# Strassen's algorithm for the first product of a fused mLSTM and feed-forward kernel, and the second product's sums by pairs of batches

## Chip, cores, metric

One core of one Trainium2 chip. The metric is device time of one execution in microseconds (us). A profile is one execution; its span is some 1.7 us shorter than the time on the clock.

## The reference

An mLSTM recurrence over 768 steps for 4 batches and 8 heads of 40 gives x, 3072 tokens by 320. A feed-forward block follows:

```python
def _moe_ref(x, w_in, w_out):          # x 3072 x 320, w_in 320 x 2048, w_out 2048 x 320
    h = x @ w_in
    g = h * (1.0 / (1.0 + np.exp(-1.702 * h)))
    return (g @ w_out).astype(np.float32)
```

Everything is f32. The kernel works in six chunks (0 to 5) of 128 steps, so 4 x 128 = 512 tokens each.

## The kernel before

For each chunk the **first product** (`up`) makes 16 tiles of 128 hidden values by 512 tokens: 256 rows of w_in are two full products of 128 rows, the other 64 rows go in pairs, two at a time. GELU takes each tile from PSUM. The **second product** (`down_fast`) uses Strassen's algorithm already: seven block products, called blocks here, for a pair of batches, two pairs, so blocks 0 to 13. The attention of the next chunk is recorded between the blocks.

```python
    def up(w, j, n, between=None, states=False):
        ...
        def full(j, first):
            for c in range(2):
                for i in range(2):
                    f = 2 * j + i
                    T.matmul(ph[j][i][:, ts], w_in_sb[:, c, f * 128:(f + 1) * 128], x[:, c, ts],
                             start=(first and c == 0), stop=(not first and c == 1))
        def rest(j, first):
            for i in range(2):
                r = slice(i * 64, i * 64 + 64)
                T.matmul(ph[j][i][:, ts], w_in_x[r, j, :], x[r, 2, ts], start=first, stop=not first)
        ...
    def hidden_sums(w, js, late):                     # both pairs of batches at once, 512 wide
        for j in js:
            ...
            if late:
                V.tensor_tensor(out=a10, in0=a00, in1=a10, op=OP.subtract)
                V.tensor_tensor(out=s4, in0=a01, in1=s2, op=OP.subtract)
            else:
                V.tensor_tensor(out=s1, in0=a10, in1=a11, op=OP.add)
                V.tensor_tensor(out=s2, in0=s1, in1=a00, op=OP.subtract)

    def down_fast(w, c):
        ...
        def product(a, b, *adds):
            po = ps_m.tile([128, DH], FP, tag="m", name="p_out")     # two PSUM banks in turn
            for f in range(NH):
                T.matmul(po, a(f), b[:, f, :], start=(f == 0), stop=(f == NH - 1))
            for dst, x in adds:                                      # VectorE frees the bank
                ...
        return [lambda: product(block(0, 0), w00, (o00, None)),
                lambda: product(total(2), t2, (o01, o00)),
                lambda: product(block(1, 0), w01, (o10, o01)),
                ...
```

The schedule is manual, and the trace shows VectorE running its instructions in the order in which they are recorded: in chunk 2 its add of block 5, whose product was over when block 6 started at 255.76, runs at 257.46, behind the 2.48 us of multiplications recorded ahead of it. `ps_m` has two banks, so block n+2 can start only when the add of block n is done (in chunk 3 the copy of block 0 ends at 319.48, and block 2 starts at 319.53).

## Time and profile before

| | before |
|---|---|
| time, median of 4 runs (lowest to highest) | 508.4 us (507.69 to 509.11) |
| PE / VectorE (DVE) / ScalarE (ACT) busy | 98% / 52% / 33% |
| chunk 3: first product, then second product with attention | 35.87 us, 44.21 us |

The last row is read from the timeline, as in the prediction, which shows the lines; the next chunk's first L432 matmul starts at 358.67. PE (the matrix engine) is busy 98% of the span and hardly waits, so a change helps if it removes matmul passes and makes no new waits.

### The profile page before, as it was taken

Reading aid. Unit: us, or ns where it says so; the run is one execution under the profiler, and the core shown is the slowest. Engines: PE = TensorE matmul, PEld = TensorE weight load, DVE = VectorE, ACT = ScalarE, POOL = GpSimd, SP = SyncE. Lnnn points to the kernel's source line nnn. Section 1 sums busy time; section 2 is a strip of 40 time slices with the busy share of each in tenths; the row PEclk is TensorE's granted clock in tenths of the full one; section 3 lists DMA queues with packets and bytes.
Section 4 is the critical chain, followed back from the end, with each engine's and each line's share of the span. In section 5 each row is a group of like instructions: output and inputs, shape, how many; then the busy total and the mean of one; then the engine's idle time right before and its main releaser. Section 6 shows DMA issues by size and latency. Waiting matters only on the chain.

```text
span 507.4 us, 9501 instructions
## 1 busy us (share of the span) xinstructions
PE 496.5 (98%) x3838; PEld 352.0 (69%) x3838; DVE 265.1 (52%) x579; ACT 167.6 (33%) x373; POOL 68.6 (14%) x109
## 2 busy tenths in 40 slices
PE   8899999999999999999999999999999999999997
PEld 4774357775448998446999445999644899744797
DVE  6879985872856741418554308465135674003511
ACT  5556766301327301224601113901132720131100
POOL 7250001321001402000322000232000120000000
PEclk9999999999999999999999999999999999999999
DMA  9999799404798403685400593500494000000000
GB/s 149 183 285 285 97 260 175 40 27 77 84 267 87 52 28 65 110 176 65 42 27 14 91 248 48 59 27 1 79 234 37 0 3 28 27 0 0 1 26 27
DMA packets 175692, 44.80 MB, mean 88 GB/s; under 512 B 164353, under 2 KB 170529, under 8 KB 175649
## 3 DMA queue, kind: packets, MB, share of 16 engines
q1 hardware_dynamic: 175648, 44.21, 46.4%
q8 instruction: 30, 0.49, 0.4%
q14 instruction: 14, 0.11, 0.1%
HBM read 40.17 MB, written 4.01 MB: 87 GB/s over the span
## 4 chain that ended last, share of the span: by engine, by line
PE 88%; DVE 7%; POOL 1%; ACT 1%; issue 1%; DVEq 0%; POOLq 0%
PE p_h L432 32%; PE p_out L533 27%; PE p_h L438 9%; PE p_out L479 7%; PE p_o L356 5%; PE p_s L345 4%; PE p_i L362 2%; PE p_x L385 1%; PE p_c L405 1%; DVE s L515 1%; DVE g L514 1%; DVE s L517 1%; DVE w_in_sb L230 1%; DVE s L518 1%; ACT g L443 1%
## 5 line engine op out<-in xcount | busy, mean ns | idle before, releaser
L432 PE MATMUL p_h<-xT,w_in_sb 128*128 128x512 f32 (+1 forms) x400 | 170.7, 580 | 2.1 <-ACT xT L386 1.2
L432 PEld LDWEIGHTS p_h<-xT,w_in_sb 128*128 128x128 f32 x400 | 74.2, 190 | 93.1 <-issue 86.5
L443 ACT ACTIVATE g<-p_h 128x512 f32<-128x512 f32 x96 | 53.5, 599 | 149.8 <-PE p_h L438 83.5
L533 PE MATMUL p_out<-w_out_sb,g 128*128 128x160 f32 x480 | 71.3, 302 | 1.5 <-DVE o_sb L536 1.5
L533 PEld LDWEIGHTS p_out<-w_out_sb,g 128*128 128x128 f32 x480 | 66.6, 190 | 5.8 <-DVE o_sb L536 2.7
L538 DVE TENSOR_TENSOR o_sb<-o_sb,p_out 128x160 f32<-128x160 f32 x70 | 21.5, 319 | 67.3 <-PE p_out L533 66.7
L386 ACT COPY xT<-p_x 128x384 f32<-128x384 f32 x24 | 11.0, 480 | 133.8 <-PE p_x L385 133.8
L517 DVE TENSOR_TENSOR s<-g 128x512 f32<-128x512 f32 x20 | 13.6, 682 | 77.4 <-ACT g L443 77.4
L334 POOL TENSOR_SCALAR_AFFINE_SELECT wt<-wt 128x1024 f32<-128x1024 f32 x24 | 26.6, 1109 | 194.8 <-DMA q_bl<-in_q_dram 101.6
L331 ACT ACTIVATE wt<-wt,cols 128x128 f32<-128x128 f32 x160 | 47.9, 392 | 0.0
L533 PE MATMUL p_out<-t,s 128*128 128x160 f32 x320 | 47.4, 301 | 0.0
L438 PE MATMUL p_h<-xT,w_in_x 64*128 64x512 f32 (+1 forms) x200 | 45.3, 588 | 0.2 <-DVE w_in_x L234 0.2
L533 PEld LDWEIGHTS p_out<-t,s 128*128 128x128 f32 x320 | 44.3, 190 | 0.5
L347 DVE TENSOR_TENSOR wt<-p_s,wt 128x512 f32<-128x512 f32 x48 | 30.5, 684 | 12.7 <-POOL wt L334 8.6
L479 PE MATMUL p_out<-w_out_sb,g 128*128 128x320 f32 x128 | 36.2, 437 | 0.0
L438 PEld LDWEIGHTS p_h<-xT,w_in_x 64*128 64x128 f32 x200 | 18.1, 186 | 22.5 <-issue 17.9
L479 PEld LDWEIGHTS p_out<-w_out_sb,g 128*128 128x128 f32 x128 | 23.8, 190 | 10.1 <-issue 0.5
L356 PE MATMUL p_o<-v_st,wt 128*64 128x41 f32 x768 | 26.8, 230 | 1.4 <-DVE wt L347 1.4
L356 PEld LDWEIGHTS p_o<-v_st,wt 128*64 128x64 f32 x768 | 24.5, 138 | 5.0 <-issue 3.2
L345 PE MATMUL p_s<-qT,kT 40*128 40x128 f32 x384 | 25.8, 280 | 0.4 <-DVE wt L347 0.4
L345 PEld LDWEIGHTS p_s<-qT,kT 40*128 40x128 f32 x384 | 22.7, 187 | 3.1 <-issue 1.1
L409 DVE TENSOR_TENSOR state<-p_c,state 40x328 f32<-40x328 f32 x16 | 7.9, 496 | 30.6 <-PE p_c L405 30.5
(117 smaller groups left out, 503.3 us busy)
## 6 DMA issues: line engine op xcount, KB each, us to landing
wt<-m_row SPq DMA_DIRECT2D x20, 512.0 KB, 6.3
bits<-in_moe_w_in_dram SPq DMA_DIRECT2D x8, 512.0 KB, 8.1
out_dram<-o_sb SPq DMA_DIRECT2D x24, 160.0 KB, 1.8
eo<-in_o_gate_dram SPq DMA_DIRECT2D x5, 640.0 KB, 6.0
v_st<-in_v_dram SPq DMA_DIRECT2D x5, 640.0 KB, 5.7
k_st<-in_k_dram SPq DMA_DIRECT2D x5, 640.0 KB, 11.0
bits<-in_moe_w_out_dram SPq DMA_DIRECT2D x8, 320.0 KB, 5.2
k_bl<-in_k_dram SPq DMA_DIRECT2D x40, 64.0 KB, 2.6
```

Source lines behind the costliest of these rows:

```text
L331: A.activation(out=x[:, h, :], in_=x[:, h, :], func=AF.Exp, scale=-1.0, bias=cols[w][:, b * H + h:b * H + h + 1])
L334: G.affine_select(out=x, in_=x, compare_op=OP.is_ge, fill=0.0, base=0, pattern=[[0, H], [1, L]], channel_multiplier=-1)
L345: T.matmul(pw[i][:, p, :], kT[w, b][r, p, :], qT[w, b][r, p, :], start=True, stop=True)
L347: V.tensor_tensor(out=wt[w, b][:, :, i, :], in0=pw[i], in1=wt[w, b][:, :, i, :], op=OP.mult)
L356: T.matmul(po[t, h, :], wt[w, b][:, p, i, t], v_st[:, b * H + h, :], start=True, stop=True)
L432: T.matmul(ph[j][i][:, ts], w_in_sb[:, c, f * 128:(f + 1) * 128], x[:, c, ts], start=(first and c == 0), stop=(not first and c == 1))
L438: T.matmul(ph[j][i][:, ts], w_in_x[r, j, :], x[r, 2, ts], start=first, stop=not first)
L443: A.activation(out=g[:, i, :], in_=ph[j][i], func=AF.Gelu_apprx_sigmoid)
L479: T.matmul(po, gs[w, f // 2][:, f % 2, b * L:(b + 1) * L], w_out_sb[:, f, :], start=(f == 0), stop=(f == NF - 1))
L517: V.tensor_tensor(out=s1, in0=a10, in1=a11, op=OP.add)
L533: T.matmul(po, a(f), b[:, f, :], start=(f == 0), stop=(f == NH - 1))
L538: V.tensor_tensor(out=dst, in0=x, in1=po, op=OP.add)
```

## The change

Intent: from chunk 2 on, the 256 full rows of the first product go by Strassen's algorithm, seven block products of 128 x 256 columns for eight. Its extra sums go to VectorE and ScalarE. The 24 KB that held the second product's sums now hold three sums of w_in as well, so there is room for one pair of batches' sums at a time: those of the first pair stay in the first product's stage, those of the second pair are made while the first pair's blocks run. The blocks get another order.

```diff
+    def up_fast(w, j, between=None):                       # four tiles a call, two calls a chunk
+        ...
+        product(chain, 0, a00, b00, True)
+        take(0, 0)                                         # ScalarE copies PSUM to g
+        product(other, 0, a01, b10, True)
+        product(chain, 0, as2, bt2)
+        take(0, 1)
+        product(other, 1, as4, b11)
+        product(chain, 0, a10, b01)
+        take(1, 1)
+        product(chain, 1, as1, bt1)
+        for k in js:
+            add(k, 0, 1, chain, 1)                         # VectorE adds PSUM to g
+        ...  # 64 rest rows, in pairs
+        for k in js:
+            add(k, 0, 0, other, 0)
+            add(k, 0, 1, other, 1)
+            A.activation(out=g[k][0], in_=g[k][0], func=AF.Gelu_apprx_sigmoid)
+        product(chain, 0, a11, bt4)
+        for k in js:
+            A.activation(out=g[k][1][:, ts[0]], in_=chain[k][:, ts[0]], func=AF.Gelu_apprx_sigmoid)
+            add(k, 1, 1, chain, 1)
+        for k in js:
+            A.activation(out=g[k][1][:, ts[1]], in_=g[k][1][:, ts[1]], func=AF.Gelu_apprx_sigmoid)
...
-        return [lambda: product(block(0, 0), w00, (o00, None)),
-                lambda: product(total(2), t2, (o01, o00)),
+        return [lambda: product(block(0, 0), w00, (o00, None), (o01, None)),
+                lambda: product(block(0, 1), w10, (o00, o00)),
+                lambda: product(summed(1), t2, (o01, o01)),
...
+            if w and j in (3, 7):                          # first pair, in the first product's stage
+                hidden_sums(w, 0, (j // 4 * 2, j // 4 * 2 + 1), 1, 2)
+                hidden_sums(w, 0, (j // 4 * 2, j // 4 * 2 + 1), 3, 4)
...
             block()
             if i in stops and side:
                 run(side.pop(0))                           # attention of the next chunk
+            if w:                                          # second pair, after blocks 4 to 7
+                for at, *what in ((4, (0, 1), 1, 2), (5, (2, 3), 1, 2), (6, range(4), 3), (7, range(4), 4)):
+                    if i == at:
+                        hidden_sums(w, 1, *what)
+            if w == 1 and i == 9:
+                first_difference()
```

More of the change, by code (lines that the diff above doesn't have):

```diff
@@ L67 @@
     gp = ctx.enter_context(tc.tile_pool(name="gp", bufs=NH))
-    sp = ctx.enter_context(tc.tile_pool(name="sp", bufs=6))
     op = ctx.enter_context(tc.tile_pool(name="op", bufs=2))
@@ L90 @@
     w_out_sb = const.tile([128, NF, DM], FP, name="w_out_sb")
+    big = const.tile([128, 6, NH * L], FP, name="big")
+    xs = const.tile([128, 3, W // 2], FP, name="xs")
     def load_gates(w):
@@ L120 @@
     w_in_bits, w_out_bits = moe_w_in.bitcast(U32), moe_w_out.bitcast(U32)
-    rest_bits = w_in_bits[256:DM, :].rearrange("k (j two m) -> two k j m", two=2, m=256)
+    rest_bits = w_in_bits[256:DM, :].rearrange("k (two m) -> two k m", two=2)
     out_bits = w_out_bits.rearrange("(f p) m -> p f m", p=128)
@@ L127, in piece_in @@
     def piece_in(c, n):
+        src = w_in_bits[c * 128:(c + 1) * 128, :].rearrange("k (two n m) -> n k two m", two=2, m=512)[n]
         return (w_in_sb[:, c, n * 512:(n + 1) * 512],
-                [(slice(0, 128), slice(0, 512), w_in_bits[c * 128:(c + 1) * 128, n * 1024:(n + 1) * 1024])])
+                [(slice(0, 128), slice(0, 512), src)])
     def piece_rest(n):
         return (w_in_x[:, n * 4:n * 4 + 4, :].rearrange("p j m -> p (j m)"),
-                [(slice(i * 64, i * 64 + 64), slice(0, 512), rest_bits[i][:, n * 4:n * 4 + 4, :]) for i in range(2)])
+                [(slice(i * 64, i * 64 + 64), slice(0, 512), rest_bits[i][:, n * 1024:(n + 1) * 1024])
+                 for i in range(2)])
     def piece_out(n):
@@ L151, in fetch @@
     def fetch(n):
-        pool = gp if 6 <= n < 10 else sp
-        bits[n] = pool.tile([128, 512, 2], U32, tag="g", name="bits")
+        if 6 <= n < 10:
+            bits[n] = gp.tile([128, 512, 2], U32, tag="g", name="bits")
+        else:
+            slot = n if n < 6 else (n - 10) % 6
+            bits[n] = big[:, slot, :].bitcast(U32).rearrange("p (a two) -> p a two", two=2)
         for r, c, src in pieces[n][1]:
@@ L216 @@
     cols, stacked, m_row, dec = {}, {}, {}, {}
-    kT, qT, wt, ys, xT, gs, o_ps, sums = {}, {}, {}, {}, {}, {}, {}, {}
+    kT, qT, wt, ys, xT, gs, o_ps = {}, {}, {}, {}, {}, {}, {}
     def convert(n, engines="AV"):
@@ L413, in carry, with hidden_of @@
             G.memset(v_st[:, :, D:D1], 1.0)
+    def hidden_of(w, j):
+        if j % 2 == 0:
+            for i in range(2):
+                gs[w, i * 4 + j // 2] = gp.tile([128, 2, W], FP, tag="g", name="g")
+        return [gs[w, i * 4 + j // 2][:, j % 2, :] for i in range(2)]
+    w_half = [[w_in_sb[:, c, :].rearrange("p (n h m) -> h p n m", h=2, m=256)[i] for c in range(2)] for i in range(2)]
     def up(w, j, n, between=None, states=False):
@@ L430, in full @@
                 for i in range(2):
-                    f = 2 * j + i
-                    T.matmul(ph[j][i][:, ts], w_in_sb[:, c, f * 128:(f + 1) * 128], x[:, c, ts],
+                    T.matmul(ph[j][i][:, ts], w_half[i][c][:, j // 2, j % 2 * 128:(j % 2 + 1) * 128], x[:, c, ts],
                              start=(first and c == 0), stop=(not first and c == 1))
@@ L440, in gelu @@
         def gelu(j):
-            g = gs[w, j] = gp.tile([128, 2, W], FP, tag="g", name="g")
-            for i in range(2):
-                A.activation(out=g[:, i, :], in_=ph[j][i], func=AF.Gelu_apprx_sigmoid)
+            for i, g in enumerate(hidden_of(w, j)):
+                A.activation(out=g, in_=ph[j][i], func=AF.Gelu_apprx_sigmoid)
         if between:
@@ L472, in up, with first_sums, first_difference, product @@
             gelu(k)
+    a00, a01, a10, a11 = w_half[0] + w_half[1]
+    as1, as2, as4 = (big[:, i, :].rearrange("p (n m) -> p n m", m=256) for i in (3, 4, 5))
+    def first_sums():
+        V.tensor_tensor(out=as1, in0=a10, in1=a11, op=OP.add)
+        V.tensor_tensor(out=as2, in0=as1, in1=a00, op=OP.subtract)
+        V.tensor_tensor(out=as4, in0=a01, in1=as2, op=OP.subtract)
+    def first_difference():
+        V.tensor_tensor(out=a10, in0=a00, in1=a10, op=OP.subtract)
+    def up_fast(w, j, between=None):
+        x = xT[w].rearrange("p c b t -> p c (b t)")
+        ts = slice(0, W // 2), slice(W // 2, W)
+        b00, b10, b01, b11 = (x[:, c, t] for t in ts for c in range(2))
+        bt1, bt2, bt4 = (xs[:, i, :] for i in range(3))
+        js = range(j, j + 4)
+        if j == 0:
+            if w + 1 < NW:
+                carry(w, (1,))
+            V.tensor_tensor(out=bt1, in0=b01, in1=b00, op=OP.subtract)
+            V.tensor_tensor(out=bt2, in0=b11, in1=bt1, op=OP.subtract)
+            V.tensor_tensor(out=b01, in0=b11, in1=b01, op=OP.subtract)
+            V.tensor_tensor(out=bt4, in0=b10, in1=bt2, op=OP.subtract)
+        if between:
+            between()
+        chain = {k: (ps_m if k - j < 2 else ps_x).tile([128, W], FP, tag="mx"[(k - j) // 2], name="p_u") for k in js}
+        other = {k: ps_a.tile([128, W], FP, tag="a", name="p_v") for k in js}
+        g = {k: hidden_of(w, k) for k in js}
+        def product(p, t, a, b, first=False):
+            for k in js:
+                T.matmul(p[k][:, ts[t]], a[:, k // 2, k % 2 * 128:(k % 2 + 1) * 128], b, start=first,
+                         stop=True, skip_group_check=True)
+        def take(i, t):
+            for k in js:
+                A.copy(out=g[k][i][:, ts[t]], in_=chain[k][:, ts[0]])
+        def add(k, i, t, p, pt):
+            V.tensor_tensor(out=g[k][i][:, ts[t]], in0=p[k][:, ts[pt]], in1=g[k][i][:, ts[t]], op=OP.add)
+        product(chain, 0, a00, b00, True)
[10 more added lines that the diff above has]
+        for k in js:
+            for i, p in enumerate((other, chain)):
+                r = slice(i * 64, i * 64 + 64)
+                T.matmul(p[k], w_in_x[r, k, :], x[r, 2, :], start=False, stop=True, skip_group_check=True)
+        for k in js:
+            add(k, 0, 0, other, 0)
+            add(k, 0, 1, other, 1)
+            A.activation(out=g[k][0], in_=g[k][0], func=AF.Gelu_apprx_sigmoid)
+        product(chain, 0, a11, bt4)
+        for k in js:
+            A.activation(out=g[k][1][:, ts[0]], in_=chain[k][:, ts[0]], func=AF.Gelu_apprx_sigmoid)
+            add(k, 1, 1, chain, 1)
+        for k in js:
+            A.activation(out=g[k][1][:, ts[1]], in_=g[k][1][:, ts[1]], func=AF.Gelu_apprx_sigmoid)
@@ L500, in weight_sums, with hidden_sums, total @@
         V.tensor_tensor(out=t4, in0=w10, in1=t2, op=OP.subtract)
-    def hidden(w, j, b):
-        return gs[w, j].rearrange("p i (c two t) -> p i c two t", two=2, t=L)[:, :, :, b, :]
-    def hidden_sums(w, js, late):
+    def hidden_sums(w, c, js, *what):
         for j in js:
-            if j % 2 == 0 and not late:
-                for x in (1, 2, 4):
-                    sums[w, x, j // 2] = sp.tile([128, 2, 2, 2, L], FP, tag="g", name="s")
-            s1, s2, s4 = (sums[w, x, j // 2][:, j % 2] for x in (1, 2, 4))
-            a00, a10, a01, a11 = hidden(w, j, 0), hidden(w, j, 1), hidden(w, j + 4, 0), hidden(w, j + 4, 1)
-            if late:
-                V.tensor_tensor(out=a10, in0=a00, in1=a10, op=OP.subtract)
-                V.tensor_tensor(out=s4, in0=a01, in1=s2, op=OP.subtract)
-            else:
-                V.tensor_tensor(out=s1, in0=a10, in1=a11, op=OP.add)
-                V.tensor_tensor(out=s2, in0=s1, in1=a00, op=OP.subtract)
+            s1, s2, s4 = (total(i)[:, 2 * j:2 * j + 2, :] for i in range(3))
+            h00, h10, h01, h11 = (gs[w, k * 4 + j][:, :, (2 * c + two) * L:(2 * c + two + 1) * L]
+                                  for k in range(2) for two in range(2))
+            for x in what:
+                out_, in0, in1, f = {1: (s1, h10, h11, OP.add), 2: (s2, s1, h00, OP.subtract),
+                                     3: (h10, h00, h10, OP.subtract), 4: (s4, h01, s2, OP.subtract)}[x]
+                V.tensor_tensor(out=out_, in0=in0, in1=in1, op=f)
+    def total(i):
+        return big[:, i, :].rearrange("p (f t) -> p f t", t=L)
     def down_fast(w, c):
@@ L525, in block, with summed @@
             return lambda f: gs[w, k * 4 + f // 2][:, f % 2, (2 * c + two) * L:(2 * c + two + 1) * L]
-        def total(x):
-            return lambda f: sums[w, x, f // 4][:, f // 2 % 2, f % 2, c, :]
+        def summed(i):
+            return lambda f: total(i)[:, f, :]
         def product(a, b, *adds):
@@ L542, in store @@
             nc.sync.dma_start(out=out[b * S + w * L:b * S + (w + 1) * L, :], in_=o[two])
-        return [lambda: product(block(0, 0), w00, (o00, None)),
-                lambda: product(total(2), t2, (o01, o00)),
+        return [lambda: product(block(0, 0), w00, (o00, None), (o01, None)),
+                lambda: product(block(0, 1), w10, (o00, o00)),
+                lambda: product(summed(1), t2, (o01, o01)),
                 lambda: product(block(1, 0), w01, (o10, o01)),
-                lambda: product(total(1), t1, (o11, o10), (o01, o01)),
-                lambda: product(block(0, 1), w10, (o00, o00)),
+                lambda: product(summed(0), t1, (o11, o10), (o01, o01)),
                 lambda: (product(block(1, 1), t4, (o10, o10)), store(1)),
-                lambda: (product(total(4), w11, (o01, o01)), store(0))]
+                lambda: (product(summed(2), w11, (o01, o01)), store(0))]
     def attention(w):
@@ L628, in weights_in, with next_keys @@
             fetch(p)
+    def next_keys():
+        gates(w + 1)
+        transposes(w + 1, 0)
+        transposes(w + 1, 1)
     for w in range(NW):
@@ L635 @@
                     if j % 4 == 0:
-                        up(w, j, 4, states=more and j == 0)
+                        if w > 1:
+                            up_fast(w, j, next_keys if more and j == 0 else None)
+                        else:
+                            up(w, j, 4, states=(j == 0))
                 elif j == 0:
@@ L653 @@
                 weight_sums()
+                first_sums()
             if more:
-                if w and j == 0:
+                if w == 1 and j == 0:
                     gates(w + 1)
@@ L666 @@
                     G.memset(q_bl, 0.0)
-                if w and 4 <= j < 6:
+                if w == 1 and 4 <= j < 6:
                     transposes(w + 1, 2 * j - 8)
                     transposes(w + 1, 2 * j - 7)
-            if w and j >= 4:
-                hidden_sums(w, (j - 4,), False)
-                if j % 2:
-                    hidden_sums(w, (j - 5, j - 4), True)
+            if w > 1 and more and j == 3:
+                transposes(w + 1, 2)
+                transposes(w + 1, 3)
+            if w and j in (3, 7):
+                hidden_sums(w, 0, (j // 4 * 2, j // 4 * 2 + 1), 1, 2)
+                hidden_sums(w, 0, (j // 4 * 2, j // 4 * 2 + 1), 3, 4)
         side = attention(w + 1) if more else []
```

## The prediction

> **What bounds the kernel now.** I read the page's busy times first, then the groups by form, then the chain that ended last in order of time, then the timeline of one steady period. Busy times:
>
> ```profile
> PE 496.5 (98%) x3838; PEld 352.0 (69%) x3838; DVE 265.1 (52%) x579; ACT 167.6 (33%) x373; POOL 68.6 (14%) x109
> ```
>
> The matmul row is busy through the whole span and the weight loads have room, so the end is set by how many matmul passes there are and how long each streams. The groups (busy us, mean ns, idle before) say which:
>
> ```profile
> L432 PE MATMUL p_h<-xT,w_in_sb 128*128 128x512 f32 x368 | 162.8, 597 | 1.5 <-DVE w_in_sb L234 0.9 <-ACT xT L386 0.6
> L432 PEld LDWEIGHTS p_h<-xT,w_in_sb 128*128 128x128 f32 x400 | 74.2, 190 | 93.1 <-issue 86.5 <-ACT xT L386 1.7 <-DVE o_sb L538 1.5
> L538 DVE TENSOR_TENSOR o_sb<-o_sb,p_out 128x160 f32<-128x160 f32 x70 | 21.5, 319 | 67.3 <-PE p_out L533 66.7
> L517 DVE TENSOR_TENSOR s<-g 128x512 f32<-128x512 f32 x20 | 13.6, 682 | 77.4 <-ACT g L443 77.4
> L443 ACT ACTIVATE g<-p_h 128x512 f32<-128x512 f32 x96 | 53.5, 599 | 149.8 <-PE p_h L438 83.5 <-PE p_h L432 66.3
> ```
>
> Each f32 matmul of the source is two recorded passes: 32 full matmuls per chunk give 64 passes. The durations overlap; the chain in order of time has the real spacing. Chunk 3's first product (start us, us, what):
>
> ```profile
> 278.75 6.87 PE p_h L432 x16
> 285.62 0.74 PE p_c L405 x32
> 286.36 3.63 PE p_h L438 x16
> 289.99 13.93 PE p_h L432 x32
> 303.92 3.63 PE p_h L438 x16
> 307.56 7.08 PE p_h L432 x16
> ```
>
> 6.87/16 = 0.429 us a pass of 512 columns. The 64-row passes run in pairs (3.63 for 8 pairs = 8 x 0.429 + 0.2). In the timeline this stage goes from the first L432 matmul at 278.59 to the first L533 matmul at 314.46, 35.87 us: 64 x 0.429 = 27.46 full, 16 x 0.429 = 6.86 rest, 0.74 state, and 0.8 left, some 0.2 at each of four changes between 128-row and 64-row passes. A whole period is 80.1 us (198.66, 278.75, 358.83 are three such starts), so the second product and the attention take 44.2.
>
> Two more places matter. First, each of the five second products has one small wait, where its third block needs the PSUM bank that VectorE frees behind the sums of the hidden values:
>
> ```profile
> 318.43 0.68 DVE L515 TENSOR_TENSOR s<-g,s 128x512 f32<-128x512 f32 x1
> 319.15 0.33 DVE L536 COPY o_sb<-p_out 128x160 f32<-128x160 f32 x1
> 319.53 2.44 PE L533 MATMUL p_out<-w_out_sb,g 128*128 128x160 f32 x16 [0.22 <-DVE o_sb L536]
> ```
>
> The block before began at 316.89 and needs 16 x 0.1356 = 2.17, so it ended at 319.06: 0.45 us lost. Second, a spot with no wait now and no slack either. After the fifth block the next chunk's attention runs; VectorE is solid from 250.11 to 257.8 and only then adds block 5 (counted from 0), which frees the bank for block 7:
>
> ```profile
> 255.07 2.48 DVE L347 TENSOR_TENSOR wt<-p_s,wt 128x512 f32<-128x512 f32 x4
> 257.46 0.31 DVE L538 TENSOR_TENSOR o_sb<-o_sb,p_out 128x160 f32<-128x160 f32 x1
> 257.93 2.34 PE L533 MATMUL p_out<-w_out_sb,g 128*128 128x160 f32 x16
> ```
>
> Block 6 began at 255.76, and 255.76 + 2.17 = 257.93: the add at 257.46 is just in time.
>
> [...] The trace has 429 ns for 512 columns[...] (the eight passes of 256 in chunk 0 take 1.92 in the chain, 8 x 0.2156 + 0.2). [...]
>
> **The change part by part.**
> Removed: one of eight block products in chunks 2 to 5. Full passes go from 64 x 0.429 = 27.46 to 7 products x 8 tiles x 2 = 112 passes x 0.2156 = 24.15: minus 3.31 a chunk. The rest rows (6.86), the state (0.74, now first) and four changes of row mode (0.8) stay.
> Added on ScalarE: three copies of 256 per tile, and GELU in three pieces instead of two: per tile 3 x 0.3 + 0.5 + 2 x 0.3 = 2.0 against 1.0, for eight tiles 16 us in 33. Added on VectorE: 32 adds from PSUM x 0.33 = 10.6 and four x differences (1.7). With gates 2.4, transposes 8 x 0.6 and half the sums (16 x 0.33) that is some 26 of 33 us. Neither becomes the bound on average.
> Inside one call of four tiles, PE: six products of 1.725 end at 10.35, rest at 13.78, the seventh at 15.5. The copies between products land within 1 us and have 1.7 until the next write to their bank. The add of product 6 for tile 0 must be done by 10.35; VectorE's other work (state, differences, gates, two transposes) ends near 8.2. So nothing waits inside a call.
> At the end of a call PE does wait. The last rest pass is readable at about 13.98; two adds of tile 3 until 14.73, its GELU of 512 until 15.4, then ScalarE's first GELU from the seventh product until 15.7, which frees the bank that the next call (or the first output block) writes: 0.3 lost. If the add on the same bank has to follow that GELU, 0.8. I take 0.5, twice a chunk: +1.0. The stage is then 24.15 + 6.86 + 0.74 + 0.8 + 1.0 = 33.55 for 35.87: minus 2.3, four times minus 9.3.
> New order of blocks: the first two need only GELU results, and the sums of the first pair (4 + 4 ops of 256, ended some 3.5 us into the block stage) are ready before the third at 4.7. The 0.45 goes five times: minus 2.2.
> Sums of the second pair: four ops stand on VectorE right behind the attention of block 4 and ahead of the add of block 5, which had no slack. They take 0.46 + 0.33 + 0.46 + 0.33 = 1.6 (two are dependent on the op ahead). The add ends at 257.77 + 1.6, so block 7 starts 1.5 late. The later groups (after blocks 5, 6, 7) fit: add 6 is ready about 0.3 before block 8 can start, and the last is over before the values of batches 2 and 3. This happens in chunks 1 to 4, where there is attention beside: 4 x 1.5 = +6.0. In chunk 5 nothing stands beside and 1.6 fits into a block.
> Once only: three sums of w_in (about 3.6 us) and a difference (1.2) on VectorE in chunk 1, in its idle time. The weight pieces come in other strides, same bytes; I count 0.
> Sum: 509.1 - 9.3 - 2.2 + 6.0 = 503.6. Since the 0.5 may be 0.3 (1.6 less over all), I put **502.8**.
>
> **The rivals.** (a) All saved passes reach the end and the sums hide: minus 13.2, minus 2.2, plus at most 2.4 at call ends gives 496 us, faster by over 2%. For it: PE is 98% busy. Against it: the add at 257.46 that ends as block 7 starts. (b) The ends of calls become the bound: if reads of one tile's bank by two engines are serialised all along, or VectorE arrives late (26 of 33 us in strict order), each call loses 1.5 to 2 and the up stage gains nothing: 8 x 1.5 = 12 more than (a), plus the 6.0: about 512. For it: twice the ScalarE work in a chain PE, VectorE, ScalarE, PE. Against it: pair by pair the adds (0.75) and GELU (0.5) fit into the 0.858 of a rest pair. (c) Smaller passes cost more than the count: were weight loads of 190 ns not hidden behind 216, 112 passes would take at least 0.24 each, +2.7 a chunk, about 514. Against it: L533 streams 160 columns at 0.1356 with the same loads.
>
> **Range and chances.** Between my sum and (a) lie 7 us, most of it the block-7 wait; above lie longer call ends, 1 us per call being 8 us. So 498.3 to 506.5. The 2% line is 498.9: faster 0.15, within 0.82, slower 0.03.
>
> **What would show it.** Right: up stage about 33.5 us in chunks 2 to 5; the 256-column passes 0.216 apart; PE waits of 0.3 to 0.8 for ScalarE or VectorE at the first product of the second call and at block 0; no wait at block 2; about 1.5 at block 7 in chunks 1 to 4, named as VectorE's add to o_sb, and none in chunk 5; a period near 78.8 for 80.1. Wrong: passes over 0.22 apart, waits inside a call, a block-7 wait that is absent or over 3, or another start of chunk 1.

Where this text gives a time that the trace before does not hold, it is the author's estimate. The trace leads to much the same. On a line through 0.1356 us for 160 columns and 0.429 for 512, a pass of 256 takes 0.2156. On a line through VectorE's 319 ns for 160 (L538) and 682 for 512 (L517), 256 take 0.42. L514 and L515 start 0.60 apart and take 0.684, which puts 256 at 0.33 apart; L518, which needs the result of L517, starts 0.73 behind it for 0.69, which puts 256 at 0.46. ScalarE's GELUs of 512 take 0.599 and start 0.49 apart (L443, four in 2.06), and its copies of 32 and 384 columns, 189 and 480 ns (L289, L386), put 256 at 0.37. ScalarE's 0.3 apart for 256 is not in it; in the changed kernel it is 0.27 (L557, four in 1.19). Nor did the trace before show that two readers of one bank follow each other, or a pass of 0.24: the 0.8 and (c) are what it would cost if so.

## The result, and the profile after

The changed kernel takes 505.76 us (median of 4 runs, 504.76 to 506.14) against 508.4 us in the same rounds. The ratio is 0.9945, interval 0.992 to 0.997: 0.55% faster, where 1.2% was predicted. A ratio here is the mean time of one kernel's fast runs over that of the other's of the same rounds, so it is not quite the ratio of the medians.

The busy line of the page after the change (busy us, share of the span, instructions):

```profile
PE 486.2 (96%) x4030; PEld 388.2 (77%) x4030; DVE 333.6 (66%) x817; ACT 204.9 (41%) x501; POOL 70.3 (14%) x109
```

PE lost 10.3 us of work (496.5 before), but the span fell by 3.0 only. So PE now waits. The chain of waits in order of time shows where, in the first call of chunk 3 (p_u is `chain`, p_v is `other`; start us, us, what):

```profile
279.82 0.74 PE p_c L413 x32
280.56 1.92 PE p_u L526 x8
282.49 1.73 PE p_v L526 x8
...
287.67 3.45 PE p_u L526 x16
...
294.79 0.77 DVE g L534 x2
295.58 0.63 ACT g L554
296.20 0.28 ACT g L557
...
296.51 0.44 DVE g L534
...
296.99 2.00 PE p_u L526 x8
```

Eight passes of 256 columns take 1.73 us, 0.216 each, as worked out, and nothing waits between the products. At the end of the call the chain leaves PE: two adds, a GELU, another GELU, another add, and only then the next call's first product. The seventh product starts at 294.69 in the timeline and streams for 1.725, to 296.42; the next starts at 296.99: 0.57 lost. At the end of the second call it is 0.58. The first product's stage is 33.73 us (279.75 to 313.48, timeline) for 35.87.

The third block of the second product no longer waits. From block 0 to the scores it was 7.44 us (314.46 to 321.90) and is 7.06 (313.48 to 320.54). The large loss comes later. The timeline of chunk 3 around blocks 6 and 7, start us and duration first, idle time and its releaser in brackets:

```profile
334.49 2.34 PE L617 MATMUL p_out<-w_out_sb,big 128*128 128x160 f32 x16
...
336.19 0.42 DVE L599 TENSOR_TENSOR big<-g 128x256 f32<-128x256 f32 x1
336.22 0.98 POOL L404 TENSOR_TENSOR state<-state,cols 128x328 f32<-128x328 f32 x1
336.64 0.84 DVE L599 TENSOR_TENSOR big<-big,g 128x256 f32<-128x256 f32 x1
...
337.85 0.42 DVE L599 TENSOR_TENSOR big<-big,g 128x256 f32<-128x256 f32 x1
338.19 0.32 DVE L622 TENSOR_TENSOR o_sb<-o_sb,p_out 128x160 f32<-128x160 f32 x1
...
338.56 0.81 PE L617 MATMUL p_out<-w_out_sb,g 128*128 128x160 f32 x4 [1.74 <-DVE o_sb L622]
```

Four sums (L599) stand ahead of the add of block 5 (L622), and block 7 starts at 338.56, right after that add. Block 6 started at 334.49; at 2.17 a block, block 7 was due at 336.66, so 1.90 us are lost. The second sum takes 0.84 where its equal, the fourth sum at 337.85, takes 0.42; at that time GpSimd scales the state, in 0.98 for its usual 0.73. Chunks 1 and 2 lose 1.90 us in the same way. Chunk 4, whose attention scales no state, has 0.42 for every sum and loses 1.49.

The account of the 3.0 us of span, from starts in the two timelines: the first product's stage -2.13, -2.14, -2.13 and -1.99 in chunks 2 to 5, together -8.4; block 0 to the scores (chunk 5: to block 3) -0.49, -0.39, -0.38, -0.60, -0.57, together -2.4; block 7 3 x 1.90 + 1.49 = +7.2; what is left, +0.6, comes in steps of 0.1: block 8 follows the late block 7 at 2.28 us, where it was 2.17, in chunks 1 to 4, and the stage behind block 13 starts 0.09 later in chunks 1 to 3.

### The profile page after: what moved, and what is told of

Its sections match the earlier page's. It is cut to its first block, busy times and chain, and to the rows that moved or that the text cites.

```text
span 504.4 us, 10239 instructions
## 1 busy us (share of the span) xinstructions
PE 486.2 (96%) x4030; PEld 388.2 (77%) x4030; DVE 333.6 (66%) x817; ACT 204.9 (41%) x501; POOL 70.3 (14%) x109
## 4 chain that ended last, share of the span: by engine, by line
PE 82%; DVE 13%; ACT 2%; POOL 1%; issue 1%; DVEq 0%; POOLq 0%
PE p_out L617 28%; PE p_u L526 11%; PE p_h L448 10%; PE p_out L567 7%; PE p_v L550 6%; PE p_v L526 5%; PE p_o L364 4%; PE p_h L454 3%; PE p_s L353 2%; DVE wt L355 2%; PE p_i L370 2%; DVE g L534 2%; DVE big L599 1%; PE p_x L393 1%; PE p_c L413 1%
## 5 line engine op out<-in xcount | busy, mean ns | idle before, releaser
L617 PEld LDWEIGHTS p_out<-w_out_sb,g 128*128 128x128 f32 x480 | 66.1, 190 | 11.3 <-DVE o_sb L622 7.5
L448 PE MATMUL p_h<-xT,w_in_sb 128*128 128x512 f32 (+1 forms) x144 | 58.1, 553 | 2.1 <-ACT xT L394 1.2
L622 DVE TENSOR_TENSOR o_sb<-o_sb,p_out 128x160 f32<-128x160 f32 x70 | 21.5, 319 | 52.6 <-PE p_out L617 52.4
L531 ACT COPY g<-p_u 128x256 f32<-128x256 f32 x96 | 34.6, 379 | 42.9 <-PE p_u L526 39.4
L448 PEld LDWEIGHTS p_h<-xT,w_in_sb 128*128 128x128 f32 x144 | 26.5, 190 | 31.5 <-issue 26.8
L617 PE MATMUL p_out<-t,big 128*128 128x160 f32 x320 | 47.5, 302 | 0.0
L617 PEld LDWEIGHTS p_out<-t,big 128*128 128x128 f32 x320 | 44.3, 190 | 0.6
L458 ACT ACTIVATE g<-p_h 128x512 f32<-128x512 f32 x32 | 17.9, 598 | 38.7 <-PE p_h L448 20.0
L526 PE MATMUL p_u<-xT,w_in_sb 128*128 128x256 f32 x128 | 31.2, 386 | 1.2 <-DVE g L534 1.2
L526 PE MATMUL p_u<-xs,big 128*128 128x256 f32 x128 | 30.2, 379 | 0.0
L550 PE MATMUL p_u<-xT,w_in_x 64*128 64x512 f32 x64 | 29.6, 602 | 0.0
L550 PE MATMUL p_v<-xT,w_in_x 64*128 64x512 f32 x64 | 29.6, 602 | 0.0
```

What stands on the lines that cost most here:

```text
L448: T.matmul(ph[j][i][:, ts], w_half[i][c][:, j // 2, j % 2 * 128:(j % 2 + 1) * 128], x[:, c, ts], start=(first and c == 0), stop=(not first ...
L526: T.matmul(p[k][:, ts[t]], a[:, k // 2, k % 2 * 128:(k % 2 + 1) * 128], b, start=first, stop=True, skip_group_check=True)
L531: A.copy(out=g[k][i][:, ts[t]], in_=chain[k][:, ts[0]])
L550: T.matmul(p[k], w_in_x[r, k, :], x[r, 2, :], start=False, stop=True, skip_group_check=True)
L622: V.tensor_tensor(out=dst, in0=x, in1=po, op=OP.add)
```

## The experiments

Theory A: the time is lost where VectorE's order puts sums ahead of an add that frees a bank, and at the ends of calls where ScalarE's GELU is recorded ahead of VectorE's add from the same bank. Rival B: VectorE has 26% more work (333.6 for 265.1 us), and a wait removed at one place turns up at another. Rival C: it is the first product's calls, their smaller passes and longer evacuation, that cost the time. Two sets of kernels ran, each beside runs of the kernel before on its own chip.

| run | median us | ratio to before | 95% interval |
|---|---|---|---|
| e1_late_sums | 501.57 | 0.9874 | 0.9853 to 0.9895 |
| e2_add_first | 502.32 | 0.9872 | 0.9853 to 0.9892 |
| e3_both | 497.86 | 0.9784 | 0.9771 to 0.9796 |
| e4_sums_alone | 513.83 | 1.0106 | 1.0089 to 1.0122 |
| e5_sums_alone_late | 506.34 | 0.9941 | 0.9924 to 0.9958 |
| e6_no_state_scale | 504.87 | 0.9918 | 0.9903 to 0.9933 |
| e7_moved_again | 495.04 | 0.9726 | 0.9708 to 0.9744 |
| e8_changed_again (control) | 506.14 | 0.9946 | 0.9928 to 0.9965 |

The kernel before had a median of 509.13 in the set of e1 to e4 and 509.10 in the other.

### e1_late_sums: the same sums, behind the add

```diff
-                for at, *what in ((4, (0, 1), 1, 2), (5, (2, 3), 1, 2), (6, range(4), 3), (7, range(4), 4)):
+                for at, *what in ((5, (0, 1), 1, 2), (6, (2, 3), 1, 2), (7, range(4), 3), (9, range(4), 4)):
```

> The changed kernel with the sums of the second pair issued after blocks 5, 6, 7 and 9 instead of 4, 5, 6 and 7; the same instructions, only VectorE's order differs. Theory A (the order on VectorE costs the time: the sums stand ahead of the add that frees block 7's bank, 1.90 us in chunks 1 to 3 and 1.49 in chunk 4): block 7 follows block 6 at 2.17 us, and the time falls by about 7.2 us to 498.6. Rival B (it is VectorE's sum of work, 334 us against 265, and the wait only moves to another block or to the end of the stage): less than 2 us gained, over 503.5.

Measured: 501.51 to 501.57 in four of six runs. Two runs, the profiled one among them, took 504.2; in that profile the 2.6 us are lost before chunk 1, in the start that no edit touches: the granted clock was 0.87 in its first 40 us, where the changed kernel's profile has 1.00. Why, I did not look into. Against the changed kernel that is 4.2 to 4.6 us, not 7.2 and not under 2. Block 7 is on time in every chunk (335.52 to 337.69 in chunk 3). But a part of the loss moved, and the timeline of chunk 1 shows to where:

```profile
193.03 0.32 DVE L622 TENSOR_TENSOR o_sb<-o_sb,p_out 128x160 f32<-128x160 f32 x1
...
193.27 2.93 DVE L599 TENSOR_TENSOR big<-g,big 128x256 f32<-128x256 f32 x4
193.41 2.44 PE L617 MATMUL p_out<-t,big 128*128 128x160 f32 x16
...
196.12 1.21 DVE L500 TENSOR_TENSOR w_in_sb<-w_in_sb 128x1024 f32<-128x1024 f32 x1
...
197.26 0.96 DVE L622 TENSOR_TENSOR o_sb<-o_sb,p_out 128x160 f32<-128x160 f32 x3
197.62 1.08 PE L617 MATMUL p_out<-t,g 128*128 128x160 f32 x6 [1.45 <-DVE o_sb L622]
```

Between the add of block 9 (193.03) and those of the next blocks (197.26) now stand the last four sums, again beside GpSimd, and chunk 1's one-off difference of w_in. Block 12 starts 4.21 us after block 11 in chunk 1 and 3.08 in chunks 2 and 3, where 2.60 is the pace without a wait: 1.61 + 2 x 0.48 = 2.6 lost, and 7.2 - 2.6 = 4.6. (Two smaller terms, some 0.4 each, cancel: block 8 follows block 7 at 2.17 again, and in chunks 1 to 3 blocks 9 and 13 start 0.05 and 0.1 later.) My choice of block 9 was the fault. This looks like rival B, so it had to be told apart from it; e7 does that.

### e2_add_first: two readers of one bank, in the other order

```diff
         for k in js:
-            A.activation(out=g[k][1][:, ts[0]], in_=chain[k][:, ts[0]], func=AF.Gelu_apprx_sigmoid)
             add(k, 1, 1, chain, 1)
+            A.activation(out=g[k][1][:, ts[0]], in_=chain[k][:, ts[0]], func=AF.Gelu_apprx_sigmoid)
```

> The changed kernel with, at the end of each call of the first product, VectorE's add from a bank recorded ahead of ScalarE's GELU from the same bank. In the trace the add waited 0.97 us for that GELU and the matrix engine lost 0.58 us per call. If the two readers of one bank are serialised by the program's order, the add now fits ahead of the GELU: loss 0.1 to 0.2 per call, eight calls, 3 us less: 502.6. If the loss is the chain of the last tile's two adds and its GELU of 512 alone, nothing changes: 505.5.

Measured: 502.32, so 3.4 to 3.8 less than the changed kernel (505.76, and 506.14 in e8). The first of the two fences is the changed kernel's timeline at the end of a call (chunk 3, first call), the second this kernel's (second call):

```profile
294.69 1.99 PE L526 MATMUL p_u<-xs,w_in_sb 128*128 128x256 f32 x8
...
296.11 1.19 ACT L557 ACTIVATE g<-p_u 128x256 f32<-128x256 f32 x4
296.51 1.09 DVE L534 TENSOR_TENSOR g<-p_u,g 128x256 f32<-128x256 f32 x3 [0.97 <-ACT g L557]
296.99 0.48 PE L526 MATMUL p_u<-xT,w_in_sb 128*128 128x256 f32 x1 [0.31 <-DVE g L534]
```

```profile
309.72 1.99 PE L526 MATMUL p_u<-xs,w_in_sb 128*128 128x256 f32 x8
...
310.49 1.68 DVE L534 TENSOR_TENSOR g<-p_u,g 128x256 f32<-128x256 f32 x4
...
311.14 1.02 ACT L558 ACTIVATE g<-p_u 128x256 f32<-128x256 f32 x3
311.56 0.68 PE L617 MATMUL p_out<-w_out_sb,g 128*128 128x160 f32 x3
```

In the changed kernel the add is idle for 0.97 until the GELU from the same bank is done, though the two read different columns. Recorded first, it runs at 310.49, without a wait, beside ScalarE's GELUs of 512, and PE loses 311.56 - (309.72 + 1.725) = 0.12 instead of 0.58. Eight calls make 3.7. The two readers take turns in the order of the program, here by a semaphore (VectorE waits 0.97 us for ScalarE's signal), and that order was the loss. A common output tile is not the reason: in the changed kernel VectorE's add at 293.07 runs without a wait for ScalarE's GELU of 293.00 to 293.63, which writes other columns of the same tile g. What the chip would do without that semaphore, no run shows.

### e3_both: both edits

> Both edits at once. If the two losses are separate (theory A and serialised readers) they add: 7.2 + 3 = 10 us less than the changed kernel, 495.5, so 0.975 of the kernel before. If one bounds the other, not below 498.

Measured: 497.86, 0.9784 of before: 7.9 to 8.3 less than the changed kernel, where the two edits alone make 4.6 + 3.7 = 8.3. So the two gains are separate and add. The number missed by 2.4 because e1's did, and it lies on the edge of the other case ("not below 498"): it is the measured gains of e1 and e2, not the number foreseen, that show the adding.

### e4_sums_alone: the other half without the first product's

```diff
-                        if w > 1:
-                            up_fast(w, j, next_keys if more and j == 0 else None)
-                        else:
-                            up(w, j, 4, states=(j == 0))
+                        up(w, j, 4, states=more and j == 0)
...  # gates and transposes of the next chunk where the kernel before has them; no sums of w_in
```

> The new sums and the new order of blocks alone, the first product with eight block products as before. Theory A: slower than the kernel before, by 4 x 1.8 for block 7, less 5 x 0.4 for the third block: plus 5 us, 513.5. Rival: if the loss came from the first product's calls (smaller passes, more ScalarE work), this kernel is at or below the kernel before, 506 to 508.5.

Measured: 513.83, 4.7 slower than before. The account gives -2.4 + 7.2 = +4.8. So rival C falls as the cause of the whole loss: without a single changed pass of the first product, the sums by pairs alone make the kernel slower, and the first product's part is worth 513.83 - 505.76 = 8.1 us. What its calls do lose at their ends is 8 x 0.58 = 4.6 us, of which e2's edit gives back 3.7.

### e7_moved_again: the last sums to a free place

```diff
-                for at, *what in ((4, (0, 1), 1, 2), (5, (2, 3), 1, 2), (6, range(4), 3), (7, range(4), 4)):
+                for at, *what in ((5, (0, 1), 1, 2), (6, (2, 3), 1, 2), (7, range(4), 3), (11, range(4), 4)):
...
-            if w == 1 and i == 9:
+            if w == 1 and i == 12:
...  # and e2's edit
```

> Both edits, with the last group of sums after block 11 instead of 9 and chunk 1's one-off difference of w_in after block 12. In e3_both block 12 starts 4.21 us after block 11 in chunk 1 and 3.08 in chunks 2 and 3, where 2.5 to 2.6 is the pace in the other kernels: 1.6 + 2 x 0.48 us lost, behind the very sums that were moved. Theory A: all of it comes back, 495.2 to 495.5, with 2.6 at block 12 in every chunk. If VectorE's sum of work were the bound, the loss would turn up at block 13 or at the next first product: 497 or more.

Measured: 495.04 (494.74 to 495.09), 0.9726 of before. The same place in chunk 1 in its timeline:

```profile
190.55 2.44 PE L617 MATMUL p_out<-t,big 128*128 128x160 f32 x16
...
193.15 2.34 PE L617 MATMUL p_out<-t,g 128*128 128x160 f32 x16
...
193.50 1.43 DVE L599 TENSOR_TENSOR big<-g,big 128x256 f32<-128x256 f32 x4
...
195.66 2.34 PE L617 MATMUL p_out<-w_out_sb,big 128*128 128x160 f32 x16
```

Blocks 11, 12 and 13 are 2.60 and 2.51 apart, and the four sums take 1.43 us, for 2.93 beside GpSimd. The trace has no wait of PE for an add left between the blocks. VectorE does all the same work (332.9 us busy against 333.6), so rival B falls: with the same instructions, the order alone was 11 us. This kernel beats the changed kernel and, by 14 us, the one before.

### e5_sums_alone_late: the halves once more, in the good order

The edit of e4 with e7's places for the sums (without e2's edit, which concerns `up_fast` only).

> The first product with eight block products as before, the new order of blocks, and the sums of the second pair after blocks 5, 6, 7 and 11. Theory A: only the gain at the third block is left, 5 x 0.4: 2 us faster than the kernel before, 507. If the new order of blocks itself costs, 509 or more.

Measured: 506.34, 2.8 faster than before. In its own trace block 0 to the scores (chunk 5: to block 3) is 0.5 shorter in chunks 1 to 3 and 0.7 in chunks 4 and 5, together 2.9. Its ratio of 0.9941 is that of the whole changed kernel, which had Strassen's first product besides. With the sums in a good place in both, that first product, with e2's edit, is worth 506.34 - 495.04 = 11.3 us.

### e6_no_state_scale: GpSimd out of the way

```diff
-        if w:
+        if w and b > 1:
             d = cols[w][...]
             ...
             G.tensor_tensor(out=old, in0=old, in1=d, op=OP.mult)      # scales the state
```

> Wrong result on purpose: the changed kernel without GpSimd's scaling of the state for batches 0 and 1. In the changed kernel the second sum after block 4 takes 0.84 us in chunks 1 to 3, where GpSimd scales the state at the same time (0.98 for its usual 0.73), and 0.42 in chunk 4, where it doesn't. If the two engines get in each other's way: 0.42 in all four chunks, the wait at block 7 1.49 everywhere, and 3 x 0.42 = 1.3 us off the changed kernel of this call. If not: 0.84 stays.

Measured: 504.87, 1.3 less than the control's 506.14 on the same chip. The result still passed the comparison: with these inputs the skipped scaling is below its tolerance. The kernel is of no use beyond the measurement. Its timeline of chunk 3:

```profile
333.32 1.43 POOL L400 TENSOR_TENSOR v_st<-v_st,cols 128x328 f32<-128x328 f32 x2
333.67 2.34 PE L617 MATMUL p_out<-w_out_sb,big 128*128 128x160 f32 x16
...
335.81 0.42 DVE L599 TENSOR_TENSOR big<-big,g 128x256 f32<-128x256 f32 x1
...
337.32 1.90 PE L617 MATMUL p_out<-w_out_sb,g 128*128 128x160 f32 x12 [1.31 <-DVE o_sb L622]
```

With GpSimd done at 334.75 the second sum takes 0.42, and block 7 loses 337.32 - (333.67 + 2.17) = 1.48. In the changed kernel's trace the second sum (two SBUF inputs) takes 0.84 beside GpSimd in chunk 3 and 0.42 without it in chunk 4; the first, beside the start of the same GpSimd instruction (336.22), takes 0.42. The multiplications of the scores (one input in PSUM) take 2.48 for four, with GpSimd busy beside them in chunk 3 and idle beside most of them in chunk 4.

### e8_changed_again: the control

> The changed kernel unaltered, as a control on the same chip: 505.8, 0.9945 of the kernel before.

Measured: 506.14, ratio 0.9946, as the first time.

## Why the prediction was wrong

The range held the time. The gain forecast was 6.3 us, 1.2%; measured were 2.6 us between the medians and 3.0 us of span, a ratio of 0.55%. The mechanisms named were found in the trace, but one was missing: GpSimd slowing one of VectorE's sums, 0.84 for 0.42. The failed step is the cost of these sums ahead of block 7; the terms of the call ends and of the stage were mis-sized too, all in the same direction.

- **Passes: right.** 0.216 us for 256 columns, nothing waits inside a call.
- **"the third block", -2.2: right.** Measured -2.4; e5 shows it alone.
- **"4 x 1.5 = +6.0" for block 7: the largest miss.** Measured 3 x 1.90 + 1.49 = 7.2. The place, the cause and the chunks were right, and chunk 4 has the very 1.5. What failed is "0.46 + 0.33 + 0.46 + 0.33 = 1.6" for the four sums: in chunks 1 to 3 the second is held up by GpSimd and the group takes 2.0, from 336.19 to 338.19 in chunk 3, where chunk 4 has 1.59. The trace of before does not show it at this place: there VectorE had only work with one SBUF input (the multiplications, 2.48 for four, and the add, 0.31), but GpSimd's scaling was in it, 255.41 to 258.2 in chunk 2, right beside 257.46. I did not ask what shares that stretch. The term is 1.2 short, and e6 recovers 1.3.
- **"I take 0.5, twice a chunk: +1.0": short, and the hedge went the wrong way.** Measured 0.57 and 0.58. I had both cases, 0.3 and 0.8, and the trace has the second one's mechanism at a smaller size; why smaller, I did not work out. Yet I moved the sum of 503.6 down to 502.8 "since the 0.5 may be 0.3". e2 shows the mechanism.
- **"minus 2.3, four times minus 9.3" for the stage: 0.9 too much.** Measured -8.4. Of the 0.9, 4 x 0.15 = 0.6 are the call ends above; chunk 5, which had no state work before either, gained least (-1.99).
- **Left over: +0.6** that I had not counted: some 0.4 at block 8 behind the late block 7 (it is gone in e1, where block 7 is on time) and some 0.3 between block 13 and the new stage (not in e4, which has the old one).

Together 1.2 + 0.9 + 0.6 - 0.2 = 2.5 of span, and 0.8 from the hedge: 3.3, which is the difference between the 6.3 forecast and the 3.0 of span.

The rivals of the prediction: (a), all saved passes reach the end, gave 496 us. It came near for another order of the same instructions: e7 measured 495.04, with call ends of 8 x 0.12 = 1.0 us where (a) allowed 2.4. (b), the calls' ends as the bound at 1.5 to 2 us each, and (c), smaller passes at 0.24, are both refuted by the trace (0.58 and 0.216). The 512 of (b) is not "12 more than (a), plus the 6.0", which makes 514; it fits only if (a)'s own 2.4 at call ends is taken out first.

## What to carry to other kernels

When an instruction is put into the stream of an engine that runs in recorded order, as VectorE did here, look at what stands behind it: an add that frees a PSUM bank and ends just in time turned nearly all that was put in front of it into time of the whole kernel (2.0 us of sums into 1.90, and 1.59 into 1.49). Such a place has no wait in the profile before, so look for it by comparing when a buffer comes free with when it is next written. Two engines that read one bank ran in the recorded order here, so record first the one that is free first (e2: 0.12 us lost at the end of a call for 0.58); and keep VectorE's sums of two SBUF inputs away from GpSimd's multiplications, which doubled one sum (0.42 to 0.84 us).
